# Two long convolutions by FFT, redesigned: twisted 2048-point transforms and an SSM kernel sampled at 641 positions

## The chip, the cores and the metric

The kernel runs on one core of a Trainium2 chip. A core has TensorE (PE, matrix multiplies), VectorE (DVE), ScalarE (ACT), GpSimd (POOL) and SyncE (SP, which here only issues transfers). The engines run their own instruction streams and wait for each other with semaphores; 16 DMA engines move data between DRAM and the on-chip memory SBUF. Matmul results land in PSUM and are copied ("evicted") to SBUF by ScalarE or VectorE. The metric is the device time of one execution in microseconds, the median of several.

## The reference

All tensors are bf16. L = 2048 positions, D = 448 channels, N = 256 modes per channel.

```python
def _A_ref(u, A_re, A_im, B_re, B_im, C_re, C_im, log_dt, Dskip):
    dt = jnp.exp(log_dt)[:, None]
    logdA = dt * (A_re + 1j * A_im)
    dB = dt * (B_re + 1j * B_im)
    P = jnp.exp(logdA[:, :, None] * l[None, None, :])       # (D, N, L)
    K = jnp.einsum("dn,dnl,dn->dl", Cc, P, dB).real         # SSM kernel (D, L)
    # y = causal convolution of u with K, by FFT of length 2L
    return y + u * Dskip

def _B_ref(q, k, v, shift_k, ssm_k, ssm_D):
    # k_shift: causal convolution of k with 4 taps per channel
    kv = k_shift * v
    # y = causal convolution of kv with ssm_k, by FFT of length 2L
    return q * (y + kv * ssm_D)

x = A_u
g = sigmoid((x * gate_w).sum(-1, keepdims=True))
out = g * _A_ref(x, ...) + (1 - g) * _B_ref(x, B_k, B_v, ...)
```

Convolution B needs no kernel to be generated. For A, the kernel K must first be generated: for every channel, 2048 sums over 256 complex exponentials.

## The kernel before

Channels are handled in two halves of 224. Each convolution half goes through: stage C (a matmul over 32 coarse positions a), stage 2 (a matmul for each of 33 frequency classes over 64 fine positions b, real and imaginary parts as separate matmuls), a pointwise complex product, stage A (the inverse of stage 2), a turn of the data through DRAM, and stage B (the inverse of stage C).

```python
def stage2(nc, psum_pool, C, S, NS, zs, consume, skip=None):
    for k in range(NCLS):                     # 33 classes
        ...
            mm(nc, pt[:, 0, :], lhsT=C[:, k, :], rhs=zr, start=True, stop=False)
            mm(nc, pt[:, 0, :], lhsT=S[:, k, :], rhs=zi, start=False, stop=(skip is None))
            if skip is not None:
                mm(nc, pt[:, 0, :], lhsT=skip[0], rhs=skip[1], start=False, stop=True)
            mm(nc, pt[:, 1, :], lhsT=C[:, k, :], rhs=zi, start=True, stop=False)
            mm(nc, pt[:, 1, :], lhsT=NS[:, k, :], rhs=zr, start=False, stop=True)

def _pointwise(nc, X, K, T):                  # six VectorE operations of 3696 elements
    V.tensor_tensor(out=T[:, 0, :], in0=x1, in1=k1, op=ALU.mult)
    ...
```

SSM kernel generation ("kgen") writes position l as l1 + 64 l2 parts: TQ holds 32 powers and TP 64 powers for each of 64 mode columns of a block, both built by repeated complex multiplication on VectorE, and a matmul per mode column sums over the modes. There are 14 blocks. The level tables E, of 12 levels, are made once by repeated squaring, written to DRAM and read back block by block; for TP each level is first expanded eightfold by ScalarE (kg_Ex).

```python
    def cmul(self, dst, src, M4, n, L, eng=None):
        P4 = self.work.tile([P, n, 2, 2, L], bf16, name=tg, tag=tg)
        V.tensor_tensor(out=P4[:], in0=in0, in1=in1, op=ALU.mult)
        self.last_dve = V.tensor_tensor(out=dst, in0=P4[:, :, :, 0, :], in1=P4[:, :, :, 1, :], op=ALU.add)

    def p_apply(Ex, n):
        for s0 in range(n):
            self.cmul(TP[:, n + s0:n + s0 + 1]..., TP[:, s0:s0 + 1]..., Ex[:]..., 1, MB * 8)
    ...
        nc.scalar.copy(TP[:, 0], pin[:].rearrange("p e c m -> p c m e"))
    ...
        for g in range(8):
            for ddl in range(4):
                for hf in range(2):
                    for comp in range(2):     # 128 matmuls a block
                        nc.tensor.matmul(pt[dg * 32:(dg + 1) * 32, ddl, h, :]...,
                                         lhsT=TQ[:, :, comp, m], rhs=TP[:, :, comp, m, :],
                                         ..., tile_position=(0, dg * 32))
```

The schedule interleaves blocks with the convolution steps by hand:

```python
        run(gB0, 1); kg_blocks(1)
        ...
        run(gA0, 1); kg_blocks(NBLK)
        run(gA0, 1)
        run(gA1, 7)
```

Before all this stand the constant tables of the transforms (33 classes of 128x128 cosines, sines and negated sines, and their transposes), the level tables, the gate, and the 4-tap convolution.

Of the kernel before, what the change touches and what calls it, by code (L numbers as in the profile page):

```python
# [13 lines left out]
i32 = mybir.dt.int32  # L14
PSUM = bass.MemoryType.PSUM
DRAM = bass.MemoryType.DRAM
TWO_PI_LO = 6.2831845
MAGIC = 12582912.0
P = 128
NCLS = 33  # L20


class Weights:

    def __init__(self, tc, pool, tmp, eng=None):
        self.tc = tc
        self.nc = tc.nc
        self.pool = pool
        self.tmp = tmp
        self.e = eng or tc.nc.gpsimd  # L30
        nc = self.nc
        pi_ = pool.tile([P, 1], i32, name="w_pidx_i")
        nc.gpsimd.iota(pi_[:], pattern=[[0, 1]], base=0, channel_multiplier=1)
        self.p_f = pool.tile([P, 1], f32, name="w_pidx_f")
        self.e.tensor_copy(self.p_f[:], pi_[:])

    def col(self, name):
        return self.tmp.tile([P, 1], f32, name=name)

    def iota_free(self, n, name, mult=1, base=0):  # L40
        nc = self.nc
        ti = self.tmp.tile([P, n], i32, name=name + "_i")
        nc.gpsimd.iota(ti[:], pattern=[[mult, n]], base=base, channel_multiplier=0)
        tf = self.tmp.tile([P, n], f32, name=name + "_f")
        self.e.tensor_copy(tf[:], ti[:])
        return tf

    def pmod(self, src_col, m, name):
        o = self.col(name)
        e = self.e  # L50
        e.tensor_scalar(out=o[:], in0=src_col[:], scalar1=1.0 / m, scalar2=-(0.5 - 0.5 / m), op0=ALU.mult, op1=ALU.add)
        e.tensor_scalar(out=o[:], in0=o[:], scalar1=MAGIC, scalar2=None, op0=ALU.add)
        e.tensor_scalar(out=o[:], in0=o[:], scalar1=-MAGIC, scalar2=None, op0=ALU.add)
        fl = self.col(name + "_fl")
        e.tensor_copy(fl[:], o[:])
        e.tensor_scalar(out=o[:], in0=o[:], scalar1=-float(m), scalar2=None, op0=ALU.mult)
        e.tensor_tensor(out=o[:], in0=o[:], in1=src_col[:], op=ALU.add)
        return o, fl

    def cos_from_q(self, out_ap, q_ap, shape):  # L60
        e = self.e
        nc = self.nc
        r = self.tmp.tile(shape, f32, name="w_r")
        qq = self.tmp.tile(shape, f32, name="w_qq")
        e.tensor_scalar(out=qq[:], in0=q_ap, scalar1=0.25, scalar2=None, op0=ALU.add)
        e.tensor_scalar(out=r[:], in0=qq[:], scalar1=MAGIC, scalar2=None, op0=ALU.add)
        e.tensor_scalar(out=r[:], in0=r[:], scalar1=-MAGIC, scalar2=None, op0=ALU.add)
        e.tensor_tensor(out=qq[:], in0=qq[:], in1=r[:], op=ALU.subtract)
        nc.scalar.activation(out_ap, qq[:], ACT.Sin, scale=TWO_PI_LO)

    def build_Wc(self):
        nc, e = self.nc, self.e
        W = self.pool.tile([P, 256], bf16, name="Wc")
        a_f, dg_f = self.pmod(self.p_f, 32, "wc_a")
        j = self.iota_free(256, "wc_j")
        zc = self.tmp.tile([P, 256], f32, name="wc_zc")
        dgj = self.tmp.tile([P, 256], f32, name="wc_dgj")
        self._fmod_free(dgj, zc, j, 4)
        ri = self.tmp.tile([P, 256], f32, name="wc_ri")
# [67 lines left out]
    def build_stageA(self, C, S, psum_pool):  # L147
# [10 lines left out]
        for (src, dst) in ((C, AC), (S, AS)):  # L158
            for k0 in range(0, NCLS, 8):
                n = min(8, NCLS - k0)  # L160
                pt = psum_pool.tile([P, 8, 128], bf16, name="ps_tr", tag="ps")
                for i in range(n):
                    nc.tensor.transpose(out=pt[:, i, :], in_=src[:, k0 + i, :], identity=ident[:])  # L163
# [54 lines left out]


NDD = 56  # L220
NHALF = 2
ND = NDD // NHALF
NCHL = ND * 4

# [622 lines left out]
```

## Time and profile before

| | |
|---|---|
| time, median of 3 | 758.75 us (757.01 to 760.3) |
| VectorE busy | 562.7 us (74%) |
| ScalarE busy | 358.1 us (47%) |
| TensorE busy | 310.4 us (41%), 3878 matmuls |
| DMA | 53.89 MB |
| mean granted TensorE clock | 0.723 |

Names in the profile are those of the program: kg_P, kg_TP, kg_TQ, kg_pin and kg_Ex belong to kgen; ps_c, ps_s, ps_a, ps_b are the PSUM tiles of stages C, 2, A and B; vd and tq are the DRAM tile of the turn and what is read back from it. L433 is line 433 of the program. A group line gives shapes as partitions x elements, the number of instructions, their busy time, the mean of one, the engine's idle time just before them, and who ended most of it. Durations of single matmuls include their latency and overlap, so their cost in a dense stretch is read from counts per microsecond.

### The profile page before, as it was taken

The page shows a single profiled execution, that of the slowest core. Times are in us where ns is not written, and L with a number is a line of the kernel's source. Part 1 is how long each engine was busy: PE and PEld are TensorE (multiplying, and loading weights), DVE is VectorE, ACT ScalarE, POOL GpSimd, SP SyncE. Part 2 cuts the span into 40 slices and gives each one's busy share as a digit, 9 for nine tenths or more (in the row PEclk, how much of TensorE's full clock was granted, in tenths as well). Part 3 has the DMA queues.
Part 4 walks back from the last instruction along what each step waited for, and adds up shares of the span by engine and source line. Part 5 has one row for each costly group of instructions (what it writes and reads, how often), then busy time and mean ns, then how long its engine had stood idle before and what let it go on. Part 6 is the DMA issues. An engine that isn't in the chain of part 4 may idle for free.

```text
span 759.5 us, 9670 instructions
## 1 busy us (share of the span) xinstructions
PE 310.4 (41%) x3878; PEld 252.7 (33%) x3878; DVE 562.7 (74%) x892; ACT 358.1 (47%) x514; POOL 12.8 (2%) x53
## 2 busy tenths in 40 slices
PE   0000003000036964074289664354448827595502
PEld 0000002000033754074267553343436726464501
DVE  4279999796698569989989599999892987325603
ACT  0425309846427392363365946334675635155200
POOL 0000000000100000000000000000000000000000
PEclk9999998555557688586595986556657777697655
DMA  1450900783811010409901104947100004600094
GB/s 43 86 102 21 227 5 0 166 225 97 173 42 42 3 42 1 90 2 174 200 1 44 42 1 101 176 99 127 14 0 2 2 0 70 125 2 1 11 183 97
DMA packets 129130, 53.89 MB, mean 71 GB/s; under 512 B 97213, under 2 KB 127293, under 8 KB 129085
## 3 DMA queue, kind: packets, MB, share of 16 engines
q1 hardware_dynamic: 65486, 22.17, 15.0%
q10 hardware_dynamic: 61582, 20.10, 14.0%
q0 software_dynamic: 2016, 11.01, 4.4%
q8 instruction: 30, 0.49, 0.3%
q14 instruction: 16, 0.12, 0.1%
HBM read 31.71 MB, written 20.19 MB: 68 GB/s over the span
## 4 chain that ended last, share of the span: by engine, by line
DVE 46%; PE 22%; ACT 15%; DMA 8%; issue 5%; ACTq 1%; DVEq 0%; SPq 0%; POOL 0%; POOLq 0%
DVE kg_P L433 15%; PE ps_s L211 10%; PE ps_kg L516 7%; DVE kg_TP L434 6%; ACT zs L585 4%; PE ps_a L211 3%; DVE kg_TQ L434 3%; DMA tq<-vd_A 2%; ACT kg_TP L499 2%; ACT kg_Ex L481 2%; DMA vd_A<-vs 2%; ACT X L667 2%; ACT xcU L789 1%; PE ps_b L211 1%; DVE kg_er L411 1%
## 5 line engine op out<-in xcount | busy, mean ns | idle before, releaser
L516 PE MATMUL ps_kg<-kg_TP,kg_TQ 128*32 128x64 bf16 x1792 | 95.8, 235 | 182.8 <-DVE kg_TP L434 182.8
L516 PEld LDWEIGHTS <-kg_TQ 128*32 128x32 bf16 x1792 | 95.0, 150 | 185.4 <-issue 184.7
L433 DVE TENSOR_TENSOR kg_P<-kg_TP,kg_Ex 128x2048 bf16<-128x2048 bf16 x98 | 120.1, 1225 | 48.0 <-ACT kg_TP L499 43.5
L481 ACT COPY kg_Ex<-kg_E 128x2048 bf16<-128x2048 bf16 x42 | 80.5, 1918 | 65.1 <-DVE kg_P L433 59.8
L211 PE MATMUL ps_s<-zs,s_C 128*128 128x112 bf16 x512 | 81.3, 237 | 27.0 <-ACT K L667 14.7
L434 DVE TENSOR_TENSOR kg_TP<-kg_P 128x1024 bf16<-128x1024 bf16 x98 | 67.8, 692 | 4.0
L433 DVE TENSOR_TENSOR kg_P<-kg_TQ,kg_E 128x2048 bf16<-128x2048 bf16 (+2 forms) x70 | 67.1, 958 | 3.1
L211 PE MATMUL ps_s<-zs,s_NS 128*128 128x112 bf16 x264 | 61.8, 239 | 0.0
L211 PE MATMUL ps_s<-zs,s_S 128*128 128x112 bf16 x248 | 58.5, 240 | 0.0
L211 PEld LDWEIGHTS <-s_C 128*128 128x128 bf16 x512 | 51.6, 108 | 11.2 <-DVE zs L591 1.2
L667 ACT CAST K<-ps_s 128x448 bf16<-128x448 f32 (+1 forms) x68 | 34.7, 522 | 41.3 <-PE ps_s L211 41.2
L211 PE MATMUL ps_a<-X,sa_C 128*128 128x112 bf16 x256 | 38.3, 234 | 38.1 <-DVE X L544 30.1
L163 PE MATMUL ps_tr<-sa_ident,s_C 128*128 128x128 bf16 x33 | 3.7, 313 | 115.8 <-DVE sa_ident L154 115.8
L585 ACT CAST xcK<-ps_kg 128x512 bf16<-128x512 f32 x14 | 8.2, 585 | 87.0 <-PE ps_kg L516 87.0
L585 ACT CAST zs<-ps_c 128x512 bf16<-128x512 f32 x84 | 44.1, 646 | 2.9 <-PE ps_c L211 2.8
L163 PEld LDWEIGHTS <-s_C 128*128 128x128 bf16 x33 | 3.4, 149 | 115.8 <-DVE sa_ident L154 115.8
L434 DVE TENSOR_TENSOR kg_TQ<-kg_P 128x1024 bf16<-128x1024 bf16 (+2 forms) x70 | 39.0, 557 | 2.1
L499 ACT COPY kg_TP<-kg_pin 128x1024 bf16<-128x1024 bf16 x14 | 27.6, 1970 | 25.0 <-DVE kg_pin L434 25.0
L211 PE MATMUL ps_b<-tq,WB 128*128 128x224 bf16 x128 | 23.4, 347 | 38.6 <-DMA tq<-vd_A 26.6
L211 PEld LDWEIGHTS <-s_S 128*128 128x128 bf16 x248 | 28.2, 114 | 18.0 <-issue 17.9
L591 DVE CAST zs<-ps_c 128x512 bf16<-128x512 f32 x14 | 9.6, 691 | 31.3 <-PE ps_c L211 17.4
L667 ACT CAST X<-ps_s 128x448 bf16<-128x448 f32 (+1 forms) x68 | 30.5, 594 | 3.4 <-PE ps_s L211 3.3
(211 smaller groups left out, 722.9 us busy)
## 6 DMA issues: line engine op xcount, KB each, us to landing
kg_E<-ed POOLq DMA_DIRECT2D x14, 768.0 KB, 5.0
ed<-E_lvl SPq DMA_DIRECT2D x7, 896.0 KB, 5.8
ed<-E_lvl ACTq DMA_DIRECT2D x5, 896.0 KB, 5.4
vd_B<-vs SPq DMA_DIRECT2D x2, 896.0 KB, 13.2
vd_B<-vs ACTq DMA_DIRECT2D x2, 896.0 KB
tq<-vd_B SPq DMA_DIRECT2D x4, 448.0 KB, 5.7
un_e<-in_A_u_dram SPq DMA_DIRECT2D x4, 448.0 KB, 9.5
tq<-vd_B ACTq DMA_DIRECT2D x4, 448.0 KB
```

Of the source, the lines that this page charges most:

```text
L163: nc.tensor.transpose(out=pt[:, i, :], in_=src[:, k0 + i, :], identity=ident[:])
L211: ins = nc.tensor.matmul(*args, **kwargs)
L411: V.tensor_tensor(out=er[:], in0=t1[:], in1=t2[:], op=ALU.subtract)
L433: V.tensor_tensor(out=P4[:], in0=in0, in1=in1, op=ALU.mult)
L434: self.last_dve = V.tensor_tensor(out=dst, in0=P4[:, :, :, 0, :], in1=P4[:, :, :, 1, :], op=ALU.add)
L481: nc.scalar.copy(Ex[:], Et[:, 3 + jj].unsqueeze(3).to_broadcast([P, 4, MB, 8]))
L499: nc.scalar.copy(TP[:, 0], pin[:].rearrange("p e c m -> p c m e"))
L516: last_mm = nc.tensor.matmul(pt[dg * 32:(dg + 1) * 32, ddl, h, :].rearrange("p (eh el) -> p eh el", eh=8), lhsT=TQ[:, :, comp, m], rhs=TP[ ...
L585: nc.scalar.copy(dst, src)
L591: V.tensor_copy(dst, src)
L667: nc.scalar.copy(dst[:, :, k:k + n, :].rearrange("p r k c -> p k r c") if n == 2 else dst[:, :, k, :], pt2[:] if n == 2 else pt2[:, 0])
L789: nc.scalar.copy(xu_v[:, q4 * 14:(q4 + 1) * 14], un_v[:, q4 * 14:(q4 + 1) * 14])
```

## The change

The whole kernel is written anew. What it does:

- Each sequence gets a complex 2048-point transform with a twist (frequencies shifted by a quarter), whose product's real part, taken back, is the first half of the linear convolution; so the padding to 4096 goes. There are 32 classes, and real and imaginary parts are the two 64-row halves of one 128-row matmul: one matmul per class and group of channels.
- A complex product becomes two VectorE multiplies by the same factor: one of the spectrum, and one of its copy with the two 64-partition halves exchanged, which is made by two SBUF-to-SBUF transfers. The sum is left to the inverse stage, which accumulates both.
- The inverse stages take the data as weights (lhsT) or keep it in place, so the turn through DRAM goes.
- The channels are handled in four groups of 112, for B and A alternately, with the kernel blocks (8 of 112 mode columns) in between. The last group of A is carried through its last stages in two halves.
- The SSM kernel is evaluated at 641 of the 2048 positions: every position up to 256, every second up to 512, every fourth up to 1024, every eighth beyond; the positions between take the value of a near one (a gather by one-hot matmuls). TQ has 21 and TP 32 powers, and the second half of TP is got from the first by one mirrored multiply.
- The level tables are made for two blocks at a time, by ScalarE's exponential and sine of a phase, just before the blocks that use them. The modes are transposed by TensorE.
- The sums of the 4-tap convolution and of the gate are made by TensorE. Constant tables are smaller and come from integer phases.
- The order of the instructions is found by the compiler's scheduler, for the whole program.

The diff is nearly the whole program; its core:

```diff
-NCLS = 33
+NV = 56
+NQG = 4
+NW = NV // NQG
+CW = 7
+NBLK = NV // CW
+M = 16 * CW
+Q_LEVELS = (4, 2, 256, 512, 1)
+P_LEVELS = (8, 16, 32, 64)
...
+def spread(nc, psum, W, zs, cols, groups, evac, room=8, tag="ps", order=None):
+    for whs in groups:
+        pt = psum.tile([P, room, 128], f32, name="ps_c", tag=tag)
+        for i, wh in enumerate(whs):
+            x = cols(wh)
+            for r in range(2):
+                nc.tensor.matmul(pt[64 * r:64 * r + 64, i, :], lhsT=x, rhs=W[:, 128 * r:128 * r + 128], start=True, stop=True,
+                                 tile_position=(0, 64 * r))
...
+        evac(zs[:].rearrange("p k (g c) -> p (k g) c", g=4)[:, :, at:at + n], pt[:, 0:n].rearrange("p i kg -> p kg i"))
+
+def transform(nc, psum, W, zs, evac, ks=range(4)):
...
+        for i in range(8):
+            k = 8 * kk + i
+            nc.tensor.matmul(pt[:, i // 4, (i % 4) * n:(i % 4 + 1) * n], lhsT=W[:, k].rearrange("p r s -> p (r s)"), rhs=zs[:, k],
+                             start=True, stop=True)
+        evac(zs[:, 8 * kk:8 * kk + 8].rearrange("p (i k) c -> p i (k c)", i=2), pt[:, :, 0:4 * n], kk % 2)
...
+def stage_a(nc, psum, pool, R, terms, evac):
...
+            for n, t in enumerate(terms):
+                nc.tensor.matmul(pt[:, i, :], lhsT=t[:].rearrange("p k (g c) -> p (k g) c", g=4)[:, :, j + i],
+                                 rhs=R[:, 128 * n:128 * n + 128], start=(n == 0), stop=(n == 1))
+        evac(U[:, :, :, j:j + m].rearrange("p r b c -> p (r b) c"), pt[:, 0:m].rearrange("p i rb -> p rb i"))
+
+def stage_b(nc, psum, G, U, consume, parts=1):
...
+            for r in range(2):
+                nc.tensor.matmul(o, lhsT=G[:, b, r].rearrange("p g a -> p (g a)"), rhs=U[:, r, b], start=(r == 0), stop=(r == 1))
...
+def products(nc, X, S, Y, k0=0, k1=32):
+    for t in (S, X):
+        nc.vector.tensor_tensor(out=fl(t), in0=fl(t), in1=fl(Y), op=ALU.mult)
...
+        q512 = mult([TQ[:, 18:19]], 512)          # KGen.block: multiplies and adds on VectorE, in one fixed order
+        p64 = mult([TP[:, 0:4]], 64)
+        add(TQ, 20, q512)
+        add(TP, 8, p64)
+        p64 = mult([TP[:, 4:8]], 64)
+        back(8, 16)
+        add(TP, 12, p64)
+        back(0, 8)
...
+                for hf in range(2):
+                    for c in range(2):
+                        for g in range(4):    # 224 matmuls a block
+                            nc.tensor.matmul(pt[32 * g:32 * g + NQ, hw, :].rearrange("p (i j) -> p i j", i=2),
+                                             lhsT=TQ[:, :, c, m], rhs=rhs, ..., tile_position=(0, 32 * g))
...
+        levels = (4, 2, 256, 1, 8, 16, 512, 32, 64)       # Tables.chunk, for two blocks
+        for i, e in enumerate(levels):
+            exps(mag[:, i], e)
+        for i, e in enumerate(levels):
+            unit(E[:, :, 0:2], e if e in P_LEVELS else -e, 0.0, 1)
+            V.tensor_tensor(out=E[:, :, 0:2], in0=E[:, :, 0:2], in1=mag[:, i]..., op=ALU.mult)
+            V.tensor_scalar(out=E[:, :, 2], in0=E[:, :, 0], scalar1=-1.0, scalar2=None, op0=ALU.mult)
...
+    seq = [("B", 0), ("B", 1), ("B", 2), ("A", 0), ("B", 3), ("A", 1), ("A", 2), ("A", 3)]
+    for j in range(NBLK - 1):
+        step(seq[j], seq[j + 1], j)
...
+    last(0, evac)
+    block(NBLK - 1)
+    last(1, evac_two)
+    stage_b(nc, psum, G, U, epilogue_A(3), 2)
...
+    with tc.block(schedule_with_timeline_sim=True):
+        body(tc, *args)
```

## The prediction

> **What bounds the kernel now.** I read the span in three stretches first, because a busy share of the whole run hides that the stages differ. Columns: stretch in us, its length, then busy us (and instructions) of each engine, the granted TensorE clock, the DMA share, GB/s.
>
> ```profile
> core 0: us, PE busy (x) PEld busy (x) DVE busy (x) ACT busy (x) POOL busy (x), PEclk, DMA share, GB/s
> 0.00:204.00 204.00, 6.36 (x66) 5.62 (x66) 154.03 (x341) 90.51 (x92) 4.18 (x18) 0.81 0.46 106
> 204.00:640.00 436.00, 244.27 (x3159) 200.70 (x3160) 368.73 (x484) 238.22 (x357) 8.65 (x35) 0.69 0.26 53
> 640.00:760.00 120.00, 59.81 (x654) 46.35 (x652) 39.94 (x68) 29.39 (x65) 0.00 (x0) 0.70 0.40 76
> ```
>
> Three different kernels: 204 us of set-up in which TensorE does 6.4 us of work; 436 us in which VectorE is the bound (368.7 of 436, 85%); 120 us in which the last half of convolution A runs alone and no engine is half busy.
>
> Next the groups of instructions, for what fills VectorE and what one costs (the figures after the bar: busy us, mean ns of one):
>
> ```profile
> L433 DVE TENSOR_TENSOR kg_P<-kg_TP,kg_Ex 128x2048 bf16<-128x2048 bf16 x98 | 120.1, 1225 | 48.0 <-ACT kg_TP L499 43.5
> L516 PE MATMUL ps_kg<-kg_TP,kg_TQ 128*32 128x64 bf16 x1792 | 95.8, 235 | 182.8 <-DVE kg_TP L434 182.8
> L434 DVE TENSOR_TENSOR kg_TP<-kg_P 128x1024 bf16<-128x1024 bf16 x98 | 67.8, 692 | 4.0
> L585 ACT CAST zs<-ps_c 128x512 bf16<-128x512 f32 x84 | 44.1, 646 | 2.9 <-PE ps_c L211 2.8
> L499 ACT COPY kg_TP<-kg_pin 128x1024 bf16<-128x1024 bf16 x14 | 27.6, 1970 | 25.0 <-DVE kg_pin L434 25.0
> ```
>
> The kernel generator's TP groups alone are 188 us of VectorE, and TensorE waits 183 us for them. All six generator groups (kg_P, kg_TP, kg_TQ, kg_pin; 120.1+67.8+67.1+39.0+19.7+13.2) are 327 us, 23.4 us for each of 14 blocks. The chain of waits agrees and names the rest:
>
> ```profile
> DVE 46%; PE 22%; ACT 15%; DMA 8%; issue 5%; ACTq 1%; DVEq 0%; SPq 0%; POOL 0%; POOLq 0%
> DVE kg_P L433 15%; PE ps_s L211 10%; PE ps_kg L516 7%; DVE kg_TP L434 6%; ACT zs L585 4%; PE ps_a L211 3%; DVE kg_TQ L434 3%; DMA tq<-vd_A 2%; ACT kg_TP L499 2%; ACT kg_Ex L481 2%; DMA vd_A<-vs 2%; ACT X L667 2%; ACT xcU L789 1%; PE ps_b L211 1%; DVE kg_er L411 1%
> ```
>
> Last, what a weight load with its matmul costs in a dense stretch, which the mean of one (latency) does not tell. Columns: stretch, length, busy (count), clock, DMA share, GB/s; then two matmuls in order of time.
>
> ```profile
> 708.50:714.50 6.00, 6.00 (x70) 0.52 0.00 0
> 601.00:607.00 6.00, 6.00 (x119) 1.00 0.01 3
> 221.00:227.00 6.00, 6.00 (x120) 0.57 0.01 3
> ```
>
> ```profile
> 714.96 0.21 PE L211 MATMUL ps_a<-X,sa_NS 128*128 128x112 bf16 x1
> 715.01 0.21 PE L211 MATMUL ps_a<-X,sa_S 128*128 128x112 bf16 x1
> ```
>
> A pair with 112 columns takes 86 ns at clock 0.52 (6.00/70) and 50 ns right after, when the clock is up. A generator pair (64 columns, 32 weight columns) takes 50 ns at clock 0.57 and at 1.00 alike: there is a floor near 50 ns for a load and a matmul.
>
> [...] the permuted copy in the groups above takes 1970 ns for 1024 elements, 1.9 ns each, against 0.83 ns where the order is kept (evictions of 224 elements take 347 ns, of 448 take 533). For PSUM no run so far shows it.
>
> **The change, part by part.** Counts are of the changed kernel's instruction lists; durations are of the rows here, scaled by elements. For VectorE I use 0.155 us + n/1920 us for bf16 in SBUF and 0.155 + n/960 for PSUM or fp32, which gives 1.22 and 0.69 at 2048 and 1024.
>
> Removed: the E tables' trip through DRAM, the kg_Ex expansion on ScalarE (80.5 us), the kg_pin permutation (27.6 us), the turn of V through DRAM (tq and vd), three big tables of 33 classes built on VectorE and transposed, the six-operation complex pointwise product.
>
> VectorE after. Generator: 26 multiplies and adds, two copies and two mirrored multiplies per block of 112 columns come to 19.0 us, times 8 blocks 152 us (327 before). Tables made per block (phases, magnitudes, negations): 80 phase operations of 0.39 [...], 36 of 0.39, 36 of 0.2 and a few more, 62 us; this is new work, though 40 squaring operations of 1.09 us go. Products 28.3+5 (14 of 2.02, 8 of 0.62; 50 before). The short convolution: 32 multiplies of 0.62 and 4 of 1.09, 24 us (32 before; its sums move to TensorE). Gate and skip about 10, epilogues 24, coefficients 12, constants 24. Sum 336 us; neighbouring short operations overlap by some 0.06 us, times 480, so about 310 (563 before).
>
> ScalarE after. Evictions: 12 input spreads of 3.7 us, 8 blocks' kernel spreads of 2.1, 15 transforms of 3.7 plus 3, eight U of 3.7, generator 13, convolution 7; tables 51 (36 magnitudes, 40 sines, 64 exponentials, of 0.3 to 0.55 each); loads of function tables and constants 25. About 250 us (358 before).
>
> TensorE after. 5297 pairs against 3878. At full clock: generator 1792 x 0.050 = 90; the last stage 1024 x 0.050 = 51 (28 columns, at the floor); spreads 896 x 0.057 = 51; transforms 544 x 0.050 = 27; inverse stage 448 x 0.057 = 26; gather 464 x 0.050 = 23; short convolution 64 x 0.2 = 13; other 6. Sum 287 us. At half clock [...] the sum is about 384. The clock was 0.69 while TensorE was 56% busy; [...] so I take 335 us. TensorE, which was third, becomes the busiest.
>
> Now along the path.
>
> Set-up. SyncE loads k, the modes, v, u and the first slice of ssm_k in this order: 1.8+1.4+1.8+1.8+0.5 MB. The like-shaped load of u landed 12.6 us after issue for 1.8 MB, so k is there at about 13 us and the slice at about 51. VectorE has 43 us up to the end of the short convolution and 42 us more to the end of the first tables; TensorE's transposes of the modes stand behind the first ssm_k transform in its order, near 60 us. So the first block starts near 90 us; now its first multiply comes after 190. Gain about 100 to 110.
>
> Steady part. From there VectorE has about 230 us left (251 by durations, less overlaps) and TensorE 335-35 = 300. TensorE bounds; if the bound engine is as busy as VectorE is now in its steady part, 85%, it takes 353 us. That replaces 436 and the 120 of the tail: the last group is a quarter of the channels, cut in halves, and has no trip through DRAM (the tq wait and vd write are 9.1+12.2+8.8 us of the chain). What is left as tail (last product, inverse stage, last stage, epilogue) is already in TensorE's order; the output's landing, about 7 us, is added.
>
> Sum: 90 + 353 + 7 = 450 us.
>
> **Rivals.** (a) VectorE stays the bound because the generator and the tables alternate with ScalarE's sines: then 310/0.85 plus set-up waits of 30 and the tail of 12 is about 405. It speaks for it that VectorE led before and that pairs of blocks with tables hold 56 to 67 us of VectorE against 75 to 90 of TensorE; that last figure speaks against. (b) Strided reads cost: the spreads and U read PSUM with the fastest index 512 bytes apart, 86,016 elements per partition; at the SBUF penalty of 1 ns more each ScalarE gets 80 us more, 330 us in all, and TensorE waits for PSUM: about 500. Against it: VectorE's epilogue reads PSUM 16 bytes apart and needs no more than its formula (444 ns for 224). (c) TensorE's strided weights (inverse stage 56 bytes apart, u and kv) load at half rate and the clock stays low: 40 to 60 us more, about 510. (d) The set-up is issue-bound: everything starts on one queue, 39 transfers at 0.3 to 2.3 us; 20 us later, about 470. (e) It gets slower, because 1400 more matmuls and small table operations eat the gain: it would need more than 300 us of new waits; nothing in the profile is of that size.
>
> **Range and chances.** (a) is the low end with some luck in the clock, 395. (b), (c) and (d) all add; two of them together give 530. I take 395 to 530, with 450 as the middle. Every sum ends far under 759, so faster by over 2% has 0.97, within 2% 0.01, slower 0.02.
>
> **What would show it.** Right: TensorE leads the busy shares (65 to 80%) and the chain of waits; generator pairs at about 50 ns; VectorE near 310, ScalarE near 250; first generator multiply near 90 us. Step (b) shows in the mean of the 128x1024 spread eviction: 1.0 us is right, near 1.9 is the rival. Step (c) shows in the count of the inverse stage per us. The time is wrong if the first block starts after 110 us, if the steady part leaves every engine under 70% busy (a chain of waits that passes between three engines), or if the generator's pairs go below the 50 ns floor because consecutive ones now go to different column groups.

## The result and the profile after

The changed kernel takes 348.66 us (346.63 to 349.22), the one before 759.52 in the same runs: a ratio of 0.459 (95% interval 0.457 to 0.461). The prediction was 450 us with a range of 395 to 530, so the time lies 46 us under the range.

First the busy times of the page of the changed kernel (us, share of the span, instructions):

```profile
PE 230.1 (66%) x5294; PEld 199.1 (57%) x5294; DVE 283.6 (82%) x610; ACT 236.5 (68%) x375; POOL 16.0 (5%) x132
```

VectorE leads, not TensorE. VectorE and ScalarE are near what was predicted (310 and 250), TensorE is 105 us under its 335. The three stretches, in the same view and with the same columns as for the kernel before:

```profile
core 0: us, PE busy (x) PEld busy (x) DVE busy (x) ACT busy (x) POOL busy (x), PEclk, DMA share, GB/s
0.00:98.00 98.00, 44.90 (x420) 29.42 (x421) 76.73 (x184) 59.15 (x87) 15.99 (x132) 0.86 0.75 117
98.00:310.00 212.00, 167.21 (x4344) 153.01 (x4343) 196.65 (x408) 166.65 (x275) 0.00 (x0) 0.80 0.16 38
310.00:348.00 38.00, 17.98 (x538) 16.64 (x535) 10.23 (x19) 10.67 (x15) 0.00 (x0) 0.59 0.29 50
```

The set-up is 98 us instead of 204, the steady part 212 instead of 436, the end 38 instead of 120. In the steady part VectorE is 93% busy and TensorE 79%. The chain that ended last (the work and waits followed back from the last instruction; shares of the span, by engine and by line) hangs on none of them alone, where before it was VectorE for 46%:

```profile
ACT 33%; PE 24%; DVE 18%; SPq 9%; DMA 8%; issue 3%; POOL 3%; DVEq 0%; ACTq 0%; POOLq 0%
ACT zs L562 10%; PE pk L368 5%; PE ps_b L273 5%; ACT zsK L562 4%; ACT ET L481 4%; PE ps_c L208 4%; ACT U L562 4%; PE ps_a L260 4%; DMA zsS<-zs 3%; SPq L625 3%; ACT ks_mag L481 3%; DVE kg_P L314 3%; DMA uu<-in_A_u_dram 3%; ACT ET L493 3%; SP
```

ScalarE's evictions (zs, zsK, U of L562) are its largest part, and no line has more than 10%. The groups of instructions (after the bar: busy us, mean ns of one, idle us before them) that answer to kg_P, kg_TP and the generator's matmuls of before:

```profile
L314 DVE TENSOR_TENSOR kg_P<-kg_TQ,ET 128x896 bf16<-128x896 bf16 (+1 forms) x64 | 43.8, 705 | 0.4
...
L368 PE MATMUL pk<-kg_TP,kg_TQ 128*21 128x32 bf16 x1792 | 29.6, 238 | 13.4 <-DVE kg_TP L324 6.9
...
L273 PE MATMUL ps_b<-U,sb_G 128*128 128x28 bf16 x1024 | 31.1, 180 | 6.4 <-ACT zs L562 3.3
```

1792 generator pairs take 29.6 us: 16.5 ns each, where the same number took 95.8 before (53.5 each). The last stage's 1024 pairs take 30 ns each. Dense stretches show it directly (stretch, length, matmuls and loads busy with their counts, clock, DMA share, GB/s). The generator first, at half clock and near full clock:

```profile
121.00:123.40 2.40, 2.40 (x163) 2.37 (x162) 0.50 0.03 7
289.00:292.00 3.00, 3.00 (x216) 3.00 (x204) 0.94 0.02 5
```

Then the last stage:

```profile
160.70:162.40 1.70, 1.70 (x64) 1.69 (x63) 0.50 0.25 64
249.50:252.50 3.00, 3.00 (x125) 3.00 (x122) 0.89 0.23 48
```

That is 14 to 15 ns for a load and a matmul of the generator and 24 to 27 ns for one of the last stage, at either clock. The prediction had a floor of 50 ns for both. The evictions of the spread, on which rival (b) rested, show no penalty for the stride in PSUM (ScalarE, shapes kept apart; the first line reads 512 bytes apart, the second in order, and both take 1.0 ns an element):

```profile
L562 ACT CAST zs<-ps_c 128x1024 bf16<-128x1024 f32 x36 | 35.6, 1040 | 7.2 <-PE ps_c L208 7.1
L562 ACT CAST zs<-ps 128x896 bf16<-128x896 f32 x48 | 41.1, 933 | 0.7 <-PE ps L221 0.7
```

### The profile page after: what moved, and what is told of

The parts are those of the page before. It is cut to its first block, busy times and chain, and to the rows that moved or that the text cites. A ratio compares the mean times of both kernels' runs of the same rounds, so it can differ in the third digit from the quotient of the medians.

```text
span 347.4 us, 11995 instructions
## 1 busy us (share of the span) xinstructions
PE 230.1 (66%) x5294; PEld 199.1 (57%) x5294; DVE 283.6 (82%) x610; ACT 236.5 (68%) x375; POOL 16.0 (5%) x132
## 4 chain that ended last, share of the span: by engine, by line
ACT 33%; PE 24%; DVE 18%; SPq 9%; DMA 8%; issue 3%; POOL 3%; DVEq 0%; ACTq 0%; POOLq 0%
ACT zs L562 10%; PE pk L368 5%; PE ps_b L273 5%; ACT zsK L562 4%; ACT ET L481 4%; PE ps_c L208 4%; ACT U L562 4%; PE ps_a L260 4%; DMA zsS<-zs 3%; SPq L625 3%; ACT ks_mag L481 3%; DVE kg_P L314 3%; DMA uu<-in_A_u_dram 3%; ACT ET L493 3%; SPq L629 2%
## 5 line engine op out<-in xcount | busy, mean ns | idle before, releaser
L562 ACT CAST zs<-ps_c 128x1024 bf16<-128x1024 f32 (+1 forms) x48 | 42.2, 936 | 7.3 <-PE ps_c L208 7.1
L314 DVE TENSOR_TENSOR kg_P<-kg_TQ,ET 128x896 bf16<-128x896 bf16 (+1 forms) x64 | 43.8, 705 | 0.4
L221 PEld LDWEIGHTS <-s_W 128*128 128x128 bf16 x480 | 30.8, 109 | 19.4 <-issue 17.8
L562 ACT CAST zs<-ps 128x896 bf16<-128x896 f32 x48 | 41.1, 933 | 0.7 <-PE ps L221 0.7
L368 PE MATMUL pk<-kg_TP,kg_TQ 128*21 128x32 bf16 x1792 | 29.6, 238 | 13.4 <-DVE kg_TP L324 6.9
L273 PE MATMUL ps_b<-U,sb_G 128*128 128x28 bf16 x1024 | 31.1, 180 | 6.4 <-ACT zs L562 3.3
L562 ACT CAST zsK<-ps_c 128x512 bf16<-128x512 f32 (+2 forms) x30 | 25.4, 852 | 13.8 <-PE ps_c L208 13.8
L273 PEld LDWEIGHTS <-sb_G 128*128 128x128 bf16 x1024 | 29.2, 100 | 9.3 <-issue 7.4
L260 PE MATMUL ps_a<-sa_R,zs 128*128 128x128 bf16 x196 | 29.6, 242 | 6.6 <-ACT zs L562 6.1
L314 DVE TENSOR_TENSOR kg_P<-kg_TP,ET 128x1792 bf16<-128x1792 bf16 (+1 forms) x32 | 30.9, 965 | 0.0
L562 ACT CAST U<-ps_a 128x1024 bf16<-128x1024 f32 (+2 forms) x30 | 27.2, 924 | 3.6 <-PE ps_a L260 3.1
L260 PE MATMUL ps_a<-sa_R,zsS 128*128 128x128 bf16 x196 | 29.3, 241 | 0.5 <-issue 0.5
L562 ACT CAST kg_S<-pk 128x448 bf16<-128x448 f32 x8 | 4.2, 527 | 25.8 <-PE pk L368 25.8
```

The costliest lines, as they stand in the source:

```text
L221: nc.tensor.matmul(pt[:, i // 4, (i % 4) * n:(i % 4 + 1) * n], lhsT=W[:, k].rearrange("p r s -> p (r s)"), rhs=zs[:, k], start=True, stop= ...
L260: nc.tensor.matmul(pt[:, i, :], lhsT=t[:].rearrange("p k (g c) -> p (k g) c", g=4)[:, :, j + i], rhs=R[:, 128 * n:128 * n + 128], start=(n ...
L273: nc.tensor.matmul(o, lhsT=G[:, b, r].rearrange("p g a -> p (g a)"), rhs=U[:, r, b], start=(r == 0), stop=(r == 1))
L314: put(V.tensor_tensor(out=P4[:, i:i + m].rearrange("p n v c m -> p n v (c m)"), in0=in0, in1=in1, op=ALU.mult))
L368: nc.tensor.matmul(pt[32 * g:32 * g + NQ, hw, :].rearrange("p (i j) -> p i j", i=2), lhsT=TQ[:, :, c, m], rhs=rhs, start=(hf == 0 and c == 0),
L562: nc.scalar.copy(dst, src)
```

## The experiments

Eighteen runs. The order tells how the reading changed: e1 and e2 tested the floor, e3 and e4 what bounds the changed kernel, and these showed that an edit also changes the order in which the scheduler issues everything; the later ones hold that order. Times are medians; differences are from 348.7 us unless said otherwise.

### The floor: column groups in turn

The new generator has the column group `g` as its innermost loop, so that consecutive pairs go to different quarters of the array; the kernel before had it outermost. Run e1 undoes that and nothing else in the program:

```diff
-            for hw in range(2 * CW):
-                h, w = divmod(hw, CW)
-                for hf in range(2):
-                    for c in range(2):
-                        for g in range(4):
+            for g in range(4):
+                for hw in range(2 * CW):
+                    h, w = divmod(hw, CW)
+                    for hf in range(2):
+                        for c in range(2):
```

> The generator's matmuls go through one 32-column group after the other (56 in a row each) instead of rotating over four with every matmul; the same 1792 pairs, the same operands. Theory R (rotation lets loads and matmuls of different column groups run at once): a pair goes from 14 ns to 35 to 50 ns, the generator's 224 pairs a block from 3.2 us to 8 to 11 us, TensorE busy up by 40 to 60 us; the time rises by 15 to 45 us, less than TensorE's gain in busy time, because VectorE bounds the steady part. Rival S (the narrower shape does it: 32 columns instead of 64, 21 weight columns instead of 32): a pair stays at 14 to 18 ns, the time within 5 us.

It takes 420.69 us (ratio 0.554, 0.553 to 0.555), +72. The same 1792 pairs take 98.8 us, 55 ns each; rate and time both lie above what theory R had named:

```profile
L368 PE MATMUL pk<-kg_TP,kg_TQ 128*21 128x32 bf16 x1792 | 98.8, 233 | 6.7 <-DVE kg_TP L324 6.7
```

Not all of the +72 is the rate. The group grew by 69 us, but the scheduler also put 490 pairs behind the last generator burst instead of 302 and went between forms of matmul 183 times instead of 117 (both are explained below).

Run e2 does the reverse in the kernel before: the same matmuls with the column group innermost.

```diff
-            for g in range(8):
-                dg, h = g // 2, g % 2
+            for h in range(2):
                 for ddl in range(4):
-                    for hf in range(2):
-                        for comp in range(2):
+                    for i in range(4):
+                        hf, comp = i // 2, i % 2
+                        for dg in range(4):
```

> The kernel before with its generator's matmuls rotated over the four column groups; nothing else changes. Theory R: a pair of 64 columns falls from 50 ns to 20 to 30 ns, 128 pairs from 6.8 to about 3 us; the matmuls of a block are 7% of the chain of waits (55 us), so the time falls by 15 to 30 us. Rival S: 50 ns as before, the time within 5 us.

It takes 736.83 us against 759.6 (ratio 0.970, 0.968 to 0.972). The group falls from 95.8 us to 29.3:

```profile
L515 PE MATMUL ps_kg<-kg_TP,kg_TQ 128*32 128x64 bf16 x1792 | 29.3, 241 | 194.3 <-DVE kg_TP L434 193.8 <-issue 0.4
```

Of 66 us saved in this group only 23 come out, because there TensorE still waits 194 us for VectorE. The floor that the prediction read off the kernel before was not one of any pair; it was one of a 32-column group used again at once. Run h3 asks for the mechanism: two groups in turn instead of four.

```diff
-            for hw in range(2 * CW):
+            for g0, hw in [(x, y) for x in (0, 2) for y in range(2 * CW)]:
                 h, w = divmod(hw, CW)
                 for hf in range(2):
                     for c in range(2):
-                        for g in range(4):
+                        for g in (g0, g0 + 1):
```

> The generator's matmuls in another order: consecutive pairs alternate between two column groups (first groups 0 and 1, then 2 and 3) instead of going round all four; same work, pairs kept together. In the changed kernel a pair takes 16.5 ns (29.6 us / 1792), with one group at a time 55 ns (98.8 us / 1792). Theory P (a column group is held some 54 ns by its load and matmul, and groups run beside each other, so the rate is 54 ns over the number of groups in turn): 27 ns a pair, 48 us for all, TensorE +17 to +20 us. Rival H (it is enough that the next load goes to any other group, whose matmul it no longer waits for): 14 to 18 ns a pair, TensorE as before. Time: by theory V +0 to +8 us; if TensorE sets the end, the 18 us in full under P.

28.6 ns a pair (all pairs over the whole span of h3: busy us and count):

```profile
0.00:376.00 376.00, 51.27 (x1792) 0.80 0.31 57
```

One group in turn 55 ns, two 28.6, four 16.5: each group is held some 55 ns and the groups run beside each other; with all four in turn that makes 14 to 16 ns. Theory P holds, rival H does not. The starts in the traces show it as well: from one pair to the next of the same group it is 57 ns (median) in e1 and in h3 and 59 in the changed kernel, and between them the other groups' pairs start a few ns apart (in the changed kernel at 145.154, 145.157, 145.160 and 145.164 us, the next four from 145.214).

A rival is that not the group but the place in PSUM is used again at once, since four pairs in a row of e1 add to one place. It falls: e1's starts are 57 ns apart whether a pair adds to the place of the one before (1344 of them) or begins a new one (440). The 57 ns do not hold for every form, though. A pair of the last stage uses all 128 columns, and so all four groups each time, and the starts are 26 ns apart (median, changed kernel); why it is not held longer no run shows.

The time of h3, 376.55 us (+28), was more than its 22 us of added work; the section on order below comes back to this.

### First tries at the bound, and a surprise

Run e3 does each of the 16 mirrored multiplies of the generator three times (+31 us of VectorE), run e4 adds two pairs ahead of each place of the last stage (1024 pairs); the results stay the same.

```diff
-            put(V.tensor_tensor(out=TP[:, 16 + i0:16 + i1], in0=src, ...))
+            for _ in range(3):
+                put(V.tensor_tensor(out=TP[:, 16 + i0:16 + i1], in0=src, ...))
```

> The changed kernel with each mirrored multiply of the generator done three times, which writes the same values again: 32 more operations of about 1.0 us start to start, 32 us of VectorE. Theory V (VectorE bounds the steady part, 197 of 212 us busy): the time rises by 26 to 34 us. Rival P (the three engines pass the work round, each with slack): by under 16 us.

```diff
+            for r in (0, 0):
+                nc.tensor.matmul(o, lhsT=G[:, b, r]..., rhs=U[:, r, b], start=True, stop=True)
             for r in range(2):
                 nc.tensor.matmul(o, lhsT=G[:, b, r]..., rhs=U[:, r, b], start=(r == 0), stop=(r == 1))
```

> The changed kernel with 1024 more pairs in the last stage (the first of each two is done three times, all with start): 24 to 27 us more of TensorE. Theory V: the time rises by under 12 us, of which 3 us stand in the tail where nothing hides them. The prediction's picture (TensorE bounds): by 20 us or more.

e3 took 392.08 us (+43 for 31 of work), more than either theory had, and e4 471.64 (+123 for some 27). In e4 TensorE's busy time rose by 127 us, and the generator's group, which e4 doesn't touch, from 29.6 to 113.7:

```profile
L370 PE MATMUL pk<-kg_TP,kg_TQ 128*21 128x32 bf16 x1792 | 113.7, 237 | 5.7 <-issue 3.8 <-DVE kg_TP L326 1.9
```

The timeline of TensorE in e4 (start, duration, line, names) shows why:

```profile
249.93 0.24 PE L370 MATMUL pk<-kg_TP,kg_TQ 128*21 128x32 bf16 x1
250.10 0.20 PE L273 MATMUL ps_b<-U,sb_G 128*128 128x28 bf16 x1
250.24 0.23 PE L370 MATMUL pk<-kg_TP,kg_TQ 128*21 128x32 bf16 x1
250.40 0.20 PE L273 MATMUL ps_b<-U,sb_G 128*128 128x28 bf16 x1
```

The scheduler had dealt generator pairs and last-stage pairs alternately. One of each takes 0.31 us (250.24 - 249.93), against 0.04 in stretches of their own: every start comes 0.14 to 0.17 us after the one before, where each is recorded to last 0.20 to 0.24, and where in a dense stretch of one form they follow every 0.014 to 0.027 us on the mean: most of the overlap is gone. Counted in the built program's order, changes between the 32-column form, the 64-column form and the full array number 117 in the changed kernel, 895 in e4 and 176 in e3. So both runs measured an order as well as a cost.

Runs f1 to f4 tried to rule that out by issuing a block's 224 generator pairs as one unit, alone (f1, the control), with the additions of e3 (f2) and e4 (f3), and with half of the transforms' evictions done twice (f4).

```diff
+            with self.tc.tile_critical():
                 for hw in range(2 * CW):
 ...
-        evac(zs[:, 8 * kk:8 * kk + 8]..., pt[:, :, 0:4 * n], kk % 2)
+        for _ in range(2 - kk % 2):                       # f4 alone
+            evac(zs[:, 8 * kk:8 * kk + 8]..., pt[:, :, 0:4 * n], kk % 2)
```

> The changed kernel with one thing pinned: the 224 generator pairs of a block are issued as one unit, so that the scheduler can put no other matmul between them. No work is added or left out. It is the control of the three runs beside it. Changes of matmul form in TensorE's order (from the 32-column generator or gather to the 64-column spread or the full array, or back) go from 117 to 80. Theory S ([...] in the run with doubled last-stage pairs the scheduler had dealt generator and last-stage pairs alternately, 895 changes, and one pair of the two took 0.30 us instead of 0.04): within 348 +- 12 us, because 117 changes at some 0.12 us are only 14 us and most lie where VectorE sets the end. Theory U (the units cost more than they save[...]): 360 to 380 us.

389.91 us (+41): theory U, and 10 us beyond its range. It looks as if the unit starts only when all its operands are there, and other matmuls wait behind it. The longest wait of f1 (us in total, times, longest) is ScalarE's for the sums; below it the same wait in the changed kernel:

```profile
ACT kg_S L563 <- PEq L360: 54.8, 8, 15.7
ACT kg_S L562 <- PE pk L368: 25.8, 5, 13.5
```

Against this control:

> As the control of this call, with the 16 mirrored multiplies of the generator done three times instead of once (+31 us of VectorE by the earlier run, the results the same). The number is the difference from the control. Theory V (VectorE sets the steady part): +24 to +36 us. Theory T (TensorE sets it, as predicted): 0 to +10 us. Theory C (a chain that passes between the engines, none of which sets it alone): +10 to +20 us. In the earlier run it was +43 us, with 176 changes of form instead of 117; theory S puts the 12 us over 31 down to them.

> As the control of this call, with 1024 further pairs in the last stage (each place written twice before the two that count; the result is the same). The number is the difference from the control. Theory S (the 123 us of the earlier run were changes of form: 895 of them; now 113): TensorE busy +24 to +35 us (26 ns a pair), and the time, with theory V, 0 to +14 us; with theory T +20 to +32 us; with theory C +8 to +18 us. Rival to S (writing one place of PSUM again and again is slow by itself): TensorE busy +90 us or more, and the time +80 us or more.

> As the control of this call, with half of the transforms' evictions done twice by ScalarE or VectorE as the kernel deals them (about 30 more of 0.92 us on ScalarE, +28 us). The number is the difference from the control. Theory V: 0 to +12 us. Theory T: 0 to +10 us, by a longer hold on PSUM. Theory C: +10 to +20 us. A ScalarE that sets the end: +24 us or more.

428.28 us (+38), 409.71 (+20) and 392.49 (+3, and not clear of noise: the four executions took 391.5 to 398.4, the control's 388.6 to 390.9). The three point at different theories: f2 lies just above theory V's range, f3 between C's and T's, f4 in V's and T's. Theory S stands: with 113 changes of form the added pairs cost TensorE 30 us of busy time, not 127, so writing one place of PSUM repeatedly was not slow by itself (28 ns a last-stage pair in f1 and f3 alike: 28.4 us for 1024 and some 58 for 2048). For the bound the control was too far from the kernel to decide: its units had made new waits, in which added work on ScalarE may have hidden (not shown).

The generator's pairs can be kept together more gently, by the highest priority for them; in the changed kernel that alters no engine's order.

```diff
-        with self.tc.high_priority():
+        with self.tc.high_priority(offset=10000000):
             pt = self.pk[:, 0:448]...
```

h3 above had this; h1 and h2 repeat e3 and e4 with it.

> The mirrored multiplies three times again (+31 us of VectorE, same results), now with the 224 generator pairs of a block given the highest priority of all, so that they stay together without being a unit that others wait for. That priority alone leaves the order of every engine of the changed kernel as it was, so the changed kernel (348.7 us) is the control. Changes of form on TensorE: 86 (changed kernel 117, first try 176). Theory V (VectorE sets the steady part): +27 to +36 us. Theory C (a chain that passes between the engines): +12 to +22 us. Theory T (TensorE sets it): 0 to +10 us. If it is +40 us or more again, the extra in the first try was not the changes of form.

> The 1024 further last-stage pairs again (same results), with the generator's pairs kept together by the same priority; 159 changes of form instead of 895. The control is the changed kernel (348.7 us, TensorE busy 230). Theory S (changes of form made the first try slow): TensorE busy 256 to 265 us. Time then: theory V +0 to +10 us, theory C +10 to +20 us, theory T +24 to +32 us.

388.79 us (+40) and 380.53 (+32). TensorE's busy time in h2 is 262, as theory S said, and yet the added work came out in full, in h1 more than in full. Two engines cannot both be the sole bound. And e3's extra over 31 us was not changes of form (86 in h1), but it might be order in another way. Run h4 showed how order can cost. It does three things in the set-up: the first slice of ssm_k is loaded ahead of v and u, k's first rows start from ScalarE's queue, and the constants of the inverse and last stages are built after the short convolution.

> The changed kernel with three moves in the set-up (same work): the first slice of ssm_k is loaded before v and u instead of after them, the four small transfers with k's first rows start from ScalarE's queue instead of SyncE's (7.1 us of its issuing), and the constants of the inverse and last stages are built after the short convolution instead of before it. Pairs of the generator kept together as in the other runs. In the changed kernel the slice lands at 53.7 us and the first generator multiply starts at 95.0 us. Theory Q (the queue's order sets the start of the first block): the slice lands near 30 us, the first generator multiply at 70 to 82 us, and the time falls by 12 to 25 us. Rival W (VectorE's and ScalarE's work in the set-up sets it: VectorE has 45 us there, ScalarE 59): the first multiply at 88 us or later, and the time falls by 0 to 8 us.

The slice was used at 36 us instead of 53.7, the first block started 8 us earlier (later than theory Q had it), and the time was 353.70 us, +5, where both theories had it fall. The last mirrored multiply of the generator (first and last start, us) in h4:

```profile
L324 DVE TENSOR_TENSOR kg_TP<-kg_TP,ET x16: 1075/1084/1093, 102.6 to 299.6; 128x1792 bf16<-128x1792 bf16 x16
```

and in the changed kernel:

```profile
L324 DVE TENSOR_TENSOR kg_TP<-kg_TP,ET x16: 1079/1082/1086, 109.4 to 306.1; 128x1792 bf16<-128x1792 bf16 x16
```

VectorE's part ends 6.5 us earlier, but what follows it is 53 us (352.3 - 299.6) instead of 41 (347.4 - 306.1). In h4's order 498 pairs stand behind the last generator burst, in the changed kernel's 302: with its priority the burst had gone ahead of the last stage of the group before, which then ran at the end, when VectorE had little left to do. In e1 and h3 the same stage stands there, too.

### The order of issue held

Runs i1, i2, i3 and i5 hold the order of TensorE, VectorE and ScalarE exactly as the scheduler gave it to the changed kernel: a table of that order, and an ordering edge without a wait from each instruction to the next. What is added stands just ahead of its own: in i1 the multiplies of e3, in i2 the pairs of e4, in i5 the evictions of f4; i3 is h3's loop.

```diff
+        for p, q in zip(order, order[1:]):
+            tc.add_manual_dep(q, p.name, <no sync>, reason="pin")
```

> The mirrored multiplies three times a third time (+31 us of VectorE, same results), now with the order of issue of TensorE, VectorE and ScalarE held exactly as in the changed kernel; the 32 added ones stand just ahead of their own. So only the work differs, and the changed kernel (348.7 us) is the control. Theory V (VectorE sets the part from 95 to 307 us, in which it is 93% busy): +28 to +34 us. Theory C (a chain that passes between the engines): +12 to +22. Theory T (TensorE): 0 to +10. Theory O (8 to 12 us of the +43 and +40 of the first tries were the scheduler's other order): as V, not +40.

> The 1024 further last-stage pairs again (same results), with all three orders of issue held as in the changed kernel and each added pair just ahead of its own. TensorE busy 255 to 262 us (230 before it). The control is the changed kernel (348.7 us). Theory V: +3 to +12 us (the fourth group's last stage, 256 of the added pairs, lies after VectorE's part and can't hide: 6 us at 26 ns). Theory C: +13 to +22. Theory T: +26 to +32. The run before, with another order, had +32 us, 35 of them after VectorE's part; if it is +26 or more again with the order held, VectorE alone does not set the time.

> The generator's pairs alternate between two column groups instead of four (28.6 ns a pair in the run before, +22 us of TensorE), all three orders of issue held as in the changed kernel. The control is the changed kernel (348.7 us). Theory V: +2 to +8 us (the last block's 224 pairs lie after VectorE's part: +2.7 us). Theory C: +10 to +16. Theory T: +20 to +24. Before, with another order: +28.

> Half of the transforms' evictions done twice by ScalarE (30 more, +26 us of ScalarE, same results), all three orders of issue held as in the changed kernel, which is the control (348.7 us). With the orders held, VectorE +31 gave +20 us and TensorE +25 gave +20. Theory C (TensorE, ScalarE and VectorE stand in one chain and none sets it alone): +13 to +24 us, the chain's share of ScalarE (33% of it) rising. Rival V2 (only VectorE and TensorE are tight; ScalarE, 68% busy, has room): 0 to +8 us. With the scheduler's own order it was +2.6.

| run | added, by the busy time of the page | time | difference |
|---|---|---|---|
| i1, VectorE | +34 us | 368.46 us | +19.8 |
| i2, TensorE | +25 us | 368.38 us | +19.7 |
| i3, TensorE (two column groups) | +15 us | 358.97 us | +10.3 |
| i5, ScalarE | +27 us | 369.28 us | +20.6 |

All four fall in the range of theory C: a cost on any of the three engines comes out for some 60 to 80% of it. For TensorE the busy time of the page hides something: the granted clock was 0.83 in i2 and 0.85 in i3 instead of 0.79, and the other matmuls took 2 and 7 us less. By their own groups i2 added 27 us and i3 22, and the shares are 74 and 47%. Each addition stands at one place in the order, so these are shares of that place and not of an engine as such. The shares of the chain show it from within; in i1

```profile
DVE 60%; ACT 14%; PE 10%; DMA 5%; issue 3%; SPq 3%; POOL 2%; DVEq 0%; ACTq 0%; POOLq 0%
```

it moves to VectorE, whose part from 93 to 330 us is now 98% busy (233.4 of 237):

```profile
93.00:330.00 237.00, 170.45 (x4372) 157.32 (x4375) 233.38 (x448) 172.81 (x285) 0.00 (x0) 0.76 0.15 35
```

VectorE had 14 us of idle time in that part of the changed kernel:

```profile
95.00:307.00 212.00, 166.06 (x4316) 151.88 (x4316) 198.32 (x414) 168.41 (x280) 0.00 (x0) 0.80 0.17 38
```

10 of them took up added work, and most of the rest of it came out. In i2 the same stretch is

```profile
93.00:322.00 229.00, 188.83 (x5175) 175.24 (x5174) 198.81 (x413) 166.72 (x275) 0.00 (x0) 0.83 0.16 37
```

VectorE's work is the same 198.8 us, spread over 229 us, and TensorE itself is idle for 40 us in it. Its idle time did not take them up, because they stand ahead of other matmuls in its order; among the waits (us, times, longest) ScalarE's for the kernel's spread is longer in i2 (first line) than in the changed kernel:

```profile
ACT zsK L564 <- PE ps_c L208: 32.8, 14, 4.5
ACT zsK L562 <- PE ps_c L208: 13.8, 13, 2.8
```

In i5 the chain's share of ScalarE rises from 33 to 44%:

```profile
ACT 44%; PE 25%; DVE 16%; issue 4%; DMA 4%; SPq 3%; POOL 2%; DVEq 0%; ACTq 0%; POOLq 0%
```

And the same edits without the order held had cost +43 and +40 (VectorE), +123 and +32 (TensorE), +28 (two groups): between 12 us and 103 of those were order. Run i4 turns this round: the set-up of h4 in h4's order up to the first generator multiply, and from there on the order of the changed kernel.

> The three moves in the set-up (the first slice of ssm_k loaded ahead of v and u, k's first rows by ScalarE's queue, constants of the inverse and last stages after the short convolution), with the order of issue of that run up to the first generator multiply and of the changed kernel after it. In that run the first multiply came at 87.5 us instead of 95.7, VectorE's part took the same 213 us, and the part after it 52 us instead of 40. Theory O (the order after the set-up took back the gain): 338 to 343 us. Rival (the later start of other things, not the order, makes the part after it longer): 347 to 355 us.

341.90 us (ratio to before 0.451, 0.450 to 0.453; the changed kernel's interval is 0.457 to 0.461): 2% under the changed kernel, and the fastest of all. In i4 the same last multiply starts at

```profile
L324 DVE TENSOR_TENSOR kg_TP<-kg_TP,ET x16: 1073/1080/1092, 101.3 to 298.4; 128x1792 bf16<-128x1792 bf16 x16
```

298.4 us, and 40.5 us follow it. The same work as h4 in another order is 11.8 us faster: theory O. No run held the order with nothing added, but from the first multiply on i4 has the work and the order of the changed kernel, and takes 251.8 us to the end (87.0 to 338.9) where that takes 252.4 (95.0 to 347.4): holding the order costs nothing by itself.

### The halves of the last group

Run e7 takes the halves away: the last group's transform, products and inverse stage come whole after the last block.

```diff
-    last(0, evac)
     block(NBLK - 1)
-    last(1, evac_two)
+    transform(nc, psum, W2, KA[3], evac)
+    U = stage_a(nc, psum, qp, R, products(nc, *XA[3], KA[3]), evac)
     stage_b(nc, psum, G, U, epilogue_A(3), 2)
```

> The changed kernel without the halves: the last channel group's transform, products and inverse stage come whole after the last block, as for the groups before it (same work in fewer and larger instructions). The order of issue is the scheduler's; by count it stands as in the changed kernel (302 pairs after the last generator burst in both, 113 changes of form against 117). Theory H (half of the last group's chain is hidden beside the last block, so that only the other half is left at the end): half of 8 evictions of 0.92 us, of the 4 products of 2.0 us and of the inverse stage come on top, +5 to +11 us. Rival (the end is set by the last generator burst and the last stage, which are there in both): -3 to +3 us.

351.05 us (ratio 0.462, 0.460 to 0.465), +2.4, in the rival's range. The two intervals touch, and the order was the scheduler's, so the halves are worth a few us at most. In the changed kernel's end VectorE waits 10.8 us for an eviction of the second half's transform and then 5.5 us for the last stage, in e7 15.1 and 7.1 (timeline of VectorE; in brackets its idle time before and who ended it):

```profile
324.46 0.62 DVE L568 CAST zsK<-ps 128x448 bf16<-128x448 f32 x1 [10.79 <-ACT zsK L566]
...
333.38 0.62 DVE L736 TENSOR_TENSOR ept<-ps_b,gt 128x448 bf16<-128x448 f32 x1 [5.49 <-PE ps_b L273]
```

The last block's spread, the transform behind it and the last stage stand in both kernels. Whether the halves bring anything with the order held was not tried.

## Why the prediction was wrong, point by point

- **What bounds before; set-up.** Right. The first generator multiply was predicted near 90 us and starts at 95.0. Rival (d), an issue-bound set-up, cost little beyond the sum: SyncE's queue is 9% of the chain, the first slice was used at 53.7 us where about 51 was predicted, and three moves in the set-up together won 7 us in i4.
- **"There is a floor near 50 ns for a load and a matmul."** This step failed. The 50 ns were read from stretches in which consecutive pairs used the same column group, and carried over to a generator that goes round four groups, to the gather and to a last stage that uses the whole array. Measured: 16.5, 25 (11.7 us over 464) and 30 ns. The rows "generator 1792 x 0.050 = 90", "the last stage 1024 x 0.050 = 51" and "gather 23" are 29.6, 31.1 and 11.7 us: 92 of the sum's 287 us were not there. Putting back the old order of the pairs (e1) gives 420.7 us, inside the predicted range; if the last stage put behind the burst costs e1 what it cost h4 (11.8 us, an estimate), 409 are left, still inside. The prediction named the column groups among the things that would make it wrong, and gave them no place in its range.
- **"TensorE, which was third, becomes the busiest" and "TensorE bounds".** Wrong, and a consequence of that floor. With it put right the prediction's own path would have had VectorE's 230 us in the lead, 230/0.85 = 271 and 368 in all (an estimate), 19 over the measured time instead of 101. The other rows (spreads 63 us, transforms 39, inverse stage 36, short convolution 18) were 24 to 46% over their full-clock figures at the granted 0.79. The step from 287 us to 335 was the author's estimate of what the clock would be; the runs do not show that denser work raises it: TensorE was busy for 66% of the span at 0.79 in the changed kernel, for 74% at 0.72 in e1 and for 76% at 0.75 in e4. Sum 230 us, not 335.
- **"300/0.85 = 353".** Measured from the first multiply to the last epilogue: 244 us (95.0 to 338.9). No engine bounds it alone: with the order held, VectorE, TensorE and ScalarE each pass on about half to four fifths of an added cost. VectorE is busy for 93% of the middle part, so dividing by 0.85 would have been too much with the right engine as well.
- **VectorE 310, ScalarE 250.** 284 and 236. The generator's part was right (152 predicted, 149 measured by its groups); the tables were taken too dear, a phase operation costs 0.27 us and not 0.39. The formula 0.155 + n/960 describes rows of the kernel before (evictions from PSUM of 224 elements in 392 ns and of 512 in 691, fp32 operations of 896 in 1084 to 1090), but not these phase operations (268 ns for 224), nor the epilogue under (b). VectorE's rows add up to 341 us and not 336, which doesn't matter here; the 384 us of TensorE at half clock were the author's estimate (the one form that the prediction measured at two clocks took 86 ns at 0.52 and 50 right after, 1.7 times as much).
- **Rivals.** (a), VectorE in the lead, had the busiest engine right and 405 us, still 56 too much: 26 us of VectorE that were not there and the 0.85. (b) fell: 1040 ns for the eviction of 1024 elements (its 86,016 elements at 1 ns would be 86 us, not 80, and the epilogue's 444 ns, called no more than the formula, are 56 over the formula's 388). (c) fell: in the changed kernel 56 inverse-stage pairs take 3.5 us at a clock of 1.00, 62 ns each, where 57 were taken. (e) was never near.

In the sum 90 + 353 + 7 the three terms measured 95, 244 and 8.4.

## What to carry to other kernels

A rate read from a dense stretch belongs to its pattern: before it is carried to new code, ask what consecutive instructions share (here a column group) and whether the new code still shares it. Going round the four column groups in the innermost loop made the generator's pairs three times as cheap for a change of loop order (95.8 us to 29.3 in e2; 98.8 in e1, which undoes it, against 29.6). When an experiment goes through a scheduler, compare the orders of issue first: here order alone moved the time by 12 to 100 us, and only with the order held did an added cost show what it is worth at its place.

## What the runs showed of the hardware

- A load and matmul of 21 to 32 weight columns: 55 ns with one column group in turn (e1), 28.6 with two (h3), 16.5 with four (changed kernel; 14.7 and 13.9 in dense stretches at clocks of 0.50 and 0.94). With four in turn, 1792 pairs that stream 32 columns took 29.6 us (changed kernel) and 1792 that stream 64 took 29.3 (e2). From pair to pair of one group it is 57 ns (median) in e1 and h3 and 59 in the changed kernel.
- A pair on the whole array with 28 columns: 24 ns (clock 0.89) and 26.6 (0.50) in dense stretches of the changed kernel, 28 over all 2048 pairs of i2, where four in a row write the same place of PSUM.
- Pairs of the two forms dealt alternately (e4): 0.31 us for one of each instead of 0.04.
- ScalarE's eviction of 1024 elements from PSUM 512 bytes apart takes 1040 ns in the changed kernel, of 896 in order 933: 1.02 and 1.04 ns an element, so this stride cost nothing. Where it writes went for more: zsK's evictions of 512 elements, written to SBUF in runs of four, take 577 to 692 ns where the run begins at an even column and 988 to 1055 at an odd one (seven each in the changed kernel; in e7, where the last one begins at an even column, it takes 600 instead of 999).
